# Sorted block attention and an FFN on one core: w_in in column halves, FFN1 pairs, a new order of the loads and of all engines' lists

## The chip, the cores and the metric

One core of one Trainium2 chip. The metric is the device time of one execution in microseconds; for the kernel before it is the median of three runs. All times in the timeline are counted from the start of the profiled span.

## The reference

`q`, `k` and `v` are `[4, 8, 768, 64]`, `sort_net` is `[4, 8, 8, 8]`. Each head's 768 tokens are 8 blocks of 96.

```python
P = sort_net
for _ in range(5):                       # row softmax, then column scaling
    P = np.exp(P - P.max(-1)); P = P / P.sum(-1); P = P / P.sum(-2)
k_sorted = einsum('bhij,bhjcd->bhicd', P, k_blocks)   # blocks mixed by P
v_sorted = einsum('bhij,bhjcd->bhicd', P, v_blocks)
attn = softmax(q_block @ k_sorted_block.T / 8)        # 96 x 96, block by block
x = (attn @ v_sorted_block)              # -> [3072 tokens, 512]
h = x @ w_in                             # w_in [512, 2048]
g = max(h, 0) + alpha * min(h, 0)
out = g @ w_out                          # w_out [2048, 512], float32
```

## The kernel before

The kernel is written as a graph of some 1,220 operations (`G.add`, with the engines that may run each, a planned duration, and the keys that it reads and writes). An order of all of them is written out by hand in the string `SEQ`; `arrange` walks through it, gives each operation its engine (the first that is allowed, or the one that a letter names: `d` for VectorE, `p` for GpSimd) and its place in that engine's list, and `emit` writes one program for each engine with the semaphore waits that the keys ask for. An entry such as `i15Y` puts 15 filler matmuls (`warm`, L1017: the identity times itself, 512 columns, into a PSUM bank that nobody reads) into TensorE's list. What stands behind a waiting instruction in an engine's list waits too.

The attention works on 32 groups `g` of 96 tokens (batch `g // 8`, block `g % 8`), all 8 heads at once. For batch 0 all preparation is done at the start:

- `load_q`, `load_k`, `load_v` go out on GpSimd's DMA queue, which also casts to bf16; then w_in (L931, four loads, one for each 128 rows), w_out (L936, two halves), and the k, v and q of batch 1 (`KS`, `VST`, `QN`).
- `sinkhorn` on VectorE, with one exponential on ScalarE in each of five rounds, makes `Pb`; `spread0` makes from it the block matrix `BDK` that mixes k and v of batch 0. `spread` makes `BDM` and `BDV` for batches 1 to 3 (L603, L613).
- `prep_q`, `prep_k` and `prep_v` are TensorE matmuls (L628, L703; for batches 1 to 3 L657 and L698) and a copy out of PSUM each (L400). Ahead of `prep_v` stand eight copies `conv_v` that regroup v; for later batches `conv_k` (L644) and `conv_v` copy into the zero-padded `KSz` and `VDz`.

In `attention(g)` there follow the scores (L741, L744), their negative maximum (L750, VectorE), the second scores with the maximum taken off (L765, L756), the exponential (L788, or L777 for batches 1 to 3, whose weights are turned by a DMA), the product with v (L797), reciprocal and scaling on VectorE (L805, L808), and the turn into `xT` (L823, or a DMA).

The FFN works on chunks of tokens: groups (0, 2) and (2, 4), 192 tokens each, then chunks of four groups, 384 tokens. `ffn1` computes one of 16 blocks of 128 hidden columns: four matmuls (L847), a negated relu into `t1` on ScalarE (L857) and a multiply-add into `hT` on VectorE (L860). Two PSUM banks (`psH`) take turns, and for the first chunk a third (`psYP`). `ffn2` (L886) sums over 16 `hT` tiles for 128 tokens, in four parts; a copy into `outstg` and a store follow.

Of the kernel before, what the change touches and what calls it, by code (L numbers as in the profile page):

```python
# [7 lines left out]
AP = bass.AP  # L8
# [24 lines left out]
0 2 11 7 3 4 1 8 9 i15Y 22 42 28 14 43 44 45 46 19 47 18 48 5 49 50 51 15 39 52 53 54 6 55 56 57 25 58 29 59  # L33
23 60 61 12 62 63 64 132 65 66 37 31 67 89 68 83 32 69 81 13 70 84 87 71 91 10 88 85 i8Y 72 40 73 90 130 74 75
86 76 133 41 77 82 78 131 92 79 i2Y 134 80 93 138 102 94d i2Y 103 26 104 147 95 105 100 148 96d 98 i4Y 99 24
101d 38 35 111a 113 97d 17 107d i2Y 158 149 106a 108d 21 159 146 i2Y 114 118 115 116 135 160 119 144 109a 124
143 125d 117 150 110a i3Y 136 145 112a i2Y 122 141 120 161 121d 30 20 123 140 36 i3Y 128 126 129d 142 151 127
137 16 139 162 152 163 164 i3G 153 165 154 183 155 166 184 i1P 167 156 157 33 i2Y 185 168 34 169 192 186 195
170 198 193 171 204 174 194 205 201 187 202 196 206 203 199 188 200 219 197 207 216 27 189 213 220 237 217 221
214 190 218 228 191 215 225 238 208 226 222 209 223 227 239 229 210 246 234 224 240 211 247 230 231 212d 235  # L40
260 253 236 290 261 241 232 248 250 242 272 262 251 249 233 291 269 252 254 270 263 350 172 255 243 292 264
271 256 258 265 293 244 312d 278 311 273 279 259d 303 337 280 266 257 245d 284 338 267 281 300 285 294 268 339
299 286 282 310 402 283 313 295 301 296 401 340 287 274 302d 304 288 314 289 347 297 309 305 315 316 298d 319
306d 317 346 341 320 378 318 307 321 322 342 308 379 325 275 323 351 324 177 343 348 326 328 175 380 327 329
355 179 349d 344 331 330 276 352 176 345d 334 381 178 353d 372 332 335 333 382 356 336 360 383 357 389 363 384
373 361 364 354 362 390 365 387 366 388d 393 385 369 367 359 386d 391 368 358 418 392 428 419 370 403 374 429
371 445 420 395 431 396d 375 430 394d 397 376 434 449 452 432 435 377 404 421 448 453 398d 436 405 447 454 181
433 399 444 458 400d 464 437 459 455 465 450 456 406 460 180 479 466 457 482 446 451d 422 182 461 423 478 483
424 476 462 407 484 467 475 477 463 494 408 474 480 495 485 481 425 504 548 486 426d 496 487 509 506 438 507d
491 505 439 488 440 492 497 535 510 493 489 524 511 441 490 515 508 442 525 512 516 534 536 517 513 468 549  # L50
414 526 469 470 521 412 514 471 537d 518 417 522 527 472d 538 523 410 519 498 560 539 499 520 545 411 409 500
542 277 546 413 561 501 540 543 550 416 502 544 562 547 415 554 541d 557 570 551 555 571 563 558 556 572 574
552 596 559 578 573 575 597 528 607 579 605 529 581 598 427 606d 608 590 530 576 580 443 591 577 582 609 583
531 625 599 637 532 584 626 610 636 564 585 587 611 569 565 627 566 634 612 592 586 635d 567 613 588 628 638
589 614 593 568 615 553 616 639d 594 503 619 617 600 620 640 601 595 661 618 641 473 621 622 602 658 623 603
676 659 645 604d 662 677 643 663 642 624 678 644 629 667 630 631 664 668 660 703 669 665 670 704 666 673 671
533 173 691 674 705 675 692 672 688 713 632 685 706 689 633d 690 712 693 686 679 687 700 717 718 701 697 714
702 694 698 715 699 723 695 748 719d 720 696 724 716 738 721 749 739 732 750 647 725 648 733 740 722 649 753
680 646 754d 729 747 681 726 741 682 730 767 776 731 727 707 734 768 683 781 735 728 769 777 708 709 778 755
751 736d 758 756 770 812 802 757 759 787 760 752 710 761 803 780 764 762 788 846 763 765 804 657 766 789 779d  # L60
651 793 653 742 805 794 782 743 784 744 654 790 795 785 745 656 783 786 771 837 791 772 650 813 773 796 838
655 774 799 797 814 825 652 798 800 792 811 815 839 801 826 816d 847 822 853 819 823 840 849 872 824 820 806
848 817 821 827 711 818 873 831 807 834 808 832 828 833 835 874 836 850 854 829d 883 857 851d 882 866 855 875
852 858 856 841 859 880 900 684 881 842 860 901 884 861 863 843 910 746 885 867 862 864 887 902 865 908 886
844 888 909d 911 891 868 889 903 892 912 893 876 913 869 809 877 890 878 914 897 915 737 894 870 879 898 934
# [10 lines left out]
1147 1142 1138 1143 1144 1151 1148 1152 1139 1153 1149 1150 1157 1140d 1220 1158 1154 1141 1159 1181 1155 1156  # L76
# [234 lines left out]
def bass_sinkhorn_attn__then__act_prelu_kernel(  # L311
# [26 lines left out]
    ANY = ("pool", "act", "dve")  # L338

# [237 lines left out]
    def spread(bs, prio):  # L577
# [24 lines left out]
        for x, b in enumerate(bs):  # L602
            G.add(DVE, lambda e, x=x, b=b: e.tensor_tensor(  # L603
                out=AP(BDM, b * 64, [[256, 128], [16, 4], [2, 8], [1, 2]]),
                in0=AP(mkhM, 0, [[8, 128], [2, 4], [0, 8], [1, 2]]),
                in1=AP(dsel, x * 8, [[48, 128], [0, 4], [1, 8], [0, 2]]), op=AluOpType.mult), 220,
                r=["dsel", "mkhM"], w=[("BDM", b)], prio=prio) if late else G.add(DVE, lambda e, x=x, b=b: e.tensor_tensor(
                out=AP(BDK, b * 128, [[512, 128], [16, 8], [2, 8], [1, 2]]),
                in0=AP(mkh, 0, [[16, 128], [2, 8], [0, 8], [1, 2]]),
                in1=AP(dsel, x * 8, [[48, 128], [0, 8], [1, 8], [0, 2]]), op=AluOpType.mult), 260,  # L610
                r=["dsel", "mkh"], w=[("BDK", b)], prio=prio)
        for x, b in enumerate(bs if late else []):
            G.add(DVE, lambda e, x=x, b=b: e.tensor_tensor(  # L613
                out=AP(BDV, b * 64, [[256, 128], [8, 8], [1, 8]]),
                in0=AP(mkhV, 0, [[8, 128], [1, 8], [0, 8]]),
                in1=AP(dsel, (n + x) * 8, [[48, 128], [0, 8], [1, 8]]), op=AluOpType.mult), 220,
# [102 lines left out]
    def attention(g, prio):  # L719
# [82 lines left out]
        if g == 1:  # L802
# [5 lines left out]
        G.add(DVE, lambda e: e.tensor_tensor(  # L808
            out=AP(xq[me], 0, [[512, 96], [256, 2], [64, 4], [1, 64]]),
            in0=AP(psZ, 0, [[1024, 96], [512, 2], [68, 4], [1, 64]]),  # L810
            in1=AP(rec[m], 0, [[8, 96], [4, 2], [1, 4], [0, 64]]), op=AluOpType.mult), t_dve(512),
            r=banks_o + [("rec", m)], w=[("xq", me)], prio=prio)
# [24 lines left out]
    def ffn1(ga, gb, ft, prio):  # L837
# [5 lines left out]

        def f(e):
            inst = None
            for kt in range(KT_TILES):
                inst = e.matmul(AP(pt, poff, [[1024, 128], [1, n]]),  # L847
                                AP(w_in_bf, kt * DFF + ft * 128, [[KT_TILES * DFF, 128], [1, 128]]),
                                AP(xT, kt * XR + tok % XR, [[KT_TILES * XR, 128], [1, n]]),
                                start=(kt == 0), stop=(kt == KT_TILES - 1))  # L850
            return inst
# [208 lines left out]
```

## Time and profile before

| what | value |
|---|---|
| median of the runs | 237.73 us (237.51 to 239.61) |
| the profiled execution | 238.1 us, span 236.4 us |
| TensorE, VectorE, ScalarE, GpSimd busy | 96%, 71%, 67%, 42% |
| granted TensorE clock | 1.0 |
| loads, size each: k, w_in, w_out, v of batch 1 | 768 KB x1, 512 KB x4, 1024 KB x2, 384 KB x2 |
| first FFN1 matmul | 29.82 us |

In the lines of the timeline the first two numbers are the start and the length; a group of matmuls has its count at the end, and in brackets stands the idle time before it and what ended it ("issue": nothing that the profile shows). Lengths of matmuls overlap, so the spacing of their starts is what one costs. PEld is the load of weights ahead of a matmul. The `q0` lines are the loads that GpSimd issues, `q8` is the queue that brings TensorE's program.

### The profile page before, as it was taken

The page shows a single profiled execution, that of the slowest core. Times are in us where ns is not written, and L with a number is a line of the kernel's source. Part 1 is how long each engine was busy: PE and PEld are TensorE (multiplying, and loading weights), DVE is VectorE, ACT ScalarE, POOL GpSimd, SP SyncE. Part 2 cuts the span into 40 slices and gives each one's busy share as a digit, 9 for nine tenths or more (in the row PEclk, how much of TensorE's full clock was granted, in tenths as well). Part 3 has the DMA queues.
Part 4 walks back from the last instruction along what each step waited for, and adds up shares of the span by engine and source line. Part 5 has one row for each costly group of instructions (what it writes and reads, how often), then busy time and mean ns, then how long its engine had stood idle before and what let it go on. Part 6 is the DMA issues. An engine that isn't in the chain of part 4 may idle for free.

```text
span 236.4 us, 6202 instructions
## 1 busy us (share of the span) xinstructions
PE 227.3 (96%) x2483; PEld 141.6 (60%) x2513; DVE 167.4 (71%) x343; ACT 158.7 (67%) x429; POOL 99.0 (42%) x144
## 2 busy tenths in 40 slices
PE   7898989999999999999999999999999999999995
PEld 3455677777666756655656565556555555555553
DVE  4764789998899988776888777566777667554420
ACT  4579456688989898676767778777676783543332
POOL 7989507934679995308999534000000000000000
PEclk9999999999999999999999999999999999999999
DMA  5999999995697998998889967594445222310023
GB/s 96 212 207 214 169 219 197 179 190 120 115 181 137 85 210 137 185 183 179 147 133 113 167 70 150 131 145 104 94 137 131 63 50 50 137 42 2 0 101 124
DMA packets 71981, 31.36 MB, mean 133 GB/s; under 512 B 64512, under 2 KB 67344, under 8 KB 71952
## 3 DMA queue, kind: packets, MB, share of 16 engines
q0 software_dynamic: 23408, 13.63, 44.3%
q1 hardware_dynamic: 48544, 17.33, 36.2%
q8 instruction: 20, 0.33, 0.6%
q14 instruction: 9, 0.07, 0.1%
HBM read 27.28 MB, written 6.29 MB: 142 GB/s over the span
## 4 chain that ended last, share of the span: by engine, by line
PE 85%; DMA 5%; ACT 4%; DVE 2%; POOL 2%; issue 2%; POOLq 0%
PE psH L847 34%; PE psYP L886 30%; DMA VST<-in_v_dram 5%; PE psS L886 4%; PE psS L741 4%; PE psO L797 3%; PE psYP L698 2%; PE psYP L657 2%; ACT hT L400 2%; PE psS L756 2%; PE psS L765 1%; PE psO L823 1%; ACT VS L400 1%; POOL VDz L484 1%; DVE nm L750 1%
## 5 line engine op out<-in xcount | busy, mean ns | idle before, releaser
L860 DVE SCALAR_TENSOR_TENSOR hT<-t,omaT,psH 128x384 bf16<-128x384 f32 (+1 forms) x139 | 77.3, 570 | 35.6 <-ACT t L857 34.4
L847 PE MATMUL psH<-xT,w_in_bf 128*128 128x384 bf16 (+1 forms) x556 | 97.9, 310 | 0.5 <-DVE rec L805 0.5
L857 ACT ACTIVATE t<-psH 128x384 f32<-128x384 f32 (+1 forms) x139 | 62.6, 462 | 41.9 <-PE psH L847 39.1
L886 PE MATMUL psYP<-w_out_bf,hT 128*128 128x512 bf16 x308 | 78.6, 379 | 1.6 <-issue 0.2
L847 PEld LDWEIGHTS psH<-xT,w_in_bf 128*128 128x128 bf16 x556 | 49.1, 98 | 29.3 <-DVE hT L860 2.3
L886 PEld LDWEIGHTS psYP<-w_out_bf,hT 128*128 128x128 bf16 x336 | 31.4, 98 | 29.7 <-ACT outstg L400 0.2
L777 ACT ACTIVATE Esb<-psS,nf 96x96 bf16<-96x96 f32 x192 | 46.2, 344 | 4.0 <-DVE nf L750 4.0
L400 POOL COPY VDz<-VST 64x384 bf16<-64x384 bf16 x40 | 33.9, 847 | 20.0 <-PE psYP L698 9.8
L644 POOL COPY KSz<-KS 64x512 bf16<-64x512 bf16 x36 | 22.1, 615 | 18.2 <-DMA KS<-in_k_dram 9.2
L750 DVE TENSOR_REDUCE nf<-psS 96x8 f32<-96x768 f32 x24 | 22.8, 951 | 4.1 <-PE psS L741 3.6
L808 DVE TENSOR_TENSOR xq<-psO,rec 96x512 bf16<-96x512 f32 x31 | 21.3, 688 | 0.7
L429 POOL DMA_DIRECT2D QN<-in_q_dram x24 | 19.8, 858 | 0.3 <-POOL QN L489 0.3
L400 ACT ACTIVATE outstg<-psYP 128x512 f32<-128x512 f32 x18 | 10.8, 598 | 5.3 <-PE psYP L886 5.1
L1017 PE MATMUL psYP<-identb 128*128 128x512 bf16 x46 | 13.3, 420 | 0.7 <-ACT identb L400 0.7
L797 PEld LDWEIGHTS psO<-VS,ET 112*128 112x128 bf16 x248 | 11.0, 98 | 3.4 <-ACT ET L788 0.3
L741 PEld LDWEIGHTS psS<-KT,QTz 128*96 128x96 bf16 x192 | 11.5, 125 | 2.1 <-ACT Esb L777 0.2
L797 PE MATMUL psO<-VS,ET 112*128 112x65 bf16 x248 | 12.7, 194 | 0.0
L741 PE MATMUL psS<-KT,QTz 128*96 128x96 bf16 x192 | 12.6, 208 | 0.0
L400 DVE CAST VS<-psYP 112x512 bf16<-112x512 f32 x15 | 10.3, 689 | 3.0 <-PE psYP L703 2.1
L698 PEld LDWEIGHTS psYP<-BDV,VDz 128*128 128x128 bf16 x192 | 8.3, 98 | 3.1 <-DVE VS L400 0.3
L805 DVE RECIPROCAL rec<-psO 96x8 f32<-96x8 f32 x31 | 6.2, 201 | 5.3 <-PE psO L797 5.2
L698 PE MATMUL psYP<-BDV,VDz 128*128 128x64 bf16 x192 | 9.5, 193 | 0.0
(139 smaller groups left out, 201.5 us busy)
## 6 DMA issues: line engine op xcount, KB each, us to landing
out_dram<-outstg SPq DMA_DIRECT2D x23, 256.0 KB, 2.4
KS<-in_k_dram POOLq DMA_DIRECT2D x3, 768.0 KB, 7.7
QN<-in_q_dram POOLq DMA_DIRECT2D x24, 96.0 KB, 6.0
w_in_bf<-in_moe_w_in_dram POOLq DMA_DIRECT2D x4, 512.0 KB, 11.2
w_out_bf<-in_moe_w_out_dram POOLq DMA_DIRECT2D x2, 1024.0 KB, 23.3
VST<-in_v_dram POOLq DMA_DIRECT2D x4, 384.0 KB, 16.0
hT<-in_q_dram POOLq DMA_DIRECT2D x1, 768.0 KB, 7.0
VST<-in_v_dram POOLq DMA_DIRECT2D x1, 768.0 KB, 10.7
```

The source lines that it names most:

```text
L400: return e.activation(o, i, ACTF.Copy) if e is nc.scalar else e.tensor_copy(o, i)
L644: G.add(POOL, lambda e, hp=hp: e.tensor_copy(AP(KSz, hp * 64 * 3072 + u % 3 * 1024 + hp * 64, [[3072, 64], [128, 8], [1, 64]]), AP(KS[n], ...
L698: inst = e.matmul(AP(t, off + dd * 64, [[row, 128], [1, 64]]), AP(VDz, (u % VSL * 8 + dd) * 128, [[VSL * 1024, 128], [1, 128]]), AP(BDV, b ...
L741: inst = e.matmul(o, AP(QTz[n], hp * 3072 + h4 * 768 + i * 96, [[6144, 128], [1, 96]]), AP(KT[n], (h4 * 8 + i) * bk, [[ld, 128], [64, 2], ...
L750: G.add(DVE, lambda e: e.tensor_reduce(AP(nx, 0, [[8, 96], [4, 2], [1, 4]]), AP(psX, 0, [[1024, 96], [512, 2], [96, 4], [1, 96]]), AxisLis ...
L777: inst = e.activation(AP(Esb[me], p * 128, [[1024, 96], [64, 2], [1, 48]]), AP(psX, (p // 4) * 512 + (p % 4) * 96, [[1024, 96], [48, 2], [ ...
L797: inst = e.matmul(AP(psZ, hp * 512 + h4 * 68, [[1024, 128], [1, 65]]), AP(ET[me] if far else ET[m], pos(h4, hp) * 96, [[800, nk], [1, 128] ...
L808: G.add(DVE, lambda e: e.tensor_tensor(out=AP(xq[me], 0, [[512, 96], [256, 2], [64, 4], [1, 64]]), in0=AP(psZ, 0, [[1024, 96], [512, 2], [ ...
L847: inst = e.matmul(AP(pt, poff, [[1024, 128], [1, n]]), AP(w_in_bf, kt * DFF + ft * 128, [[KT_TILES * DFF, 128], [1, 128]]), AP(xT, kt * XR ...
L857: G.add(ACT, lambda e: e.activation(AP(t1[tb], 0, [[384, 128], [1, n]]), AP(pt, poff, [[1024, 128], [1, n]]), ACTF.Relu, scale=-1.0), t_ac ...
L860: G.add(DVE, lambda e: e.scalar_tensor_tensor(out=AP(hT, ft * RING + tok % RING, [[FT_TILES * RING, 128], [1, n]]), in0=AP(t1[tb], 0, [[38 ...
L886: inst = e.matmul(AP(bank[0], bank[1], [[1024, 128], [1, n]]), AP(hT, ft * RING + tok % RING, [[FT_TILES * RING, 128], [1, 128]]), AP(w_ou ...
```

## The change

- `w_in` is still loaded in four pieces, but each is half of the columns of two row blocks (4 KB runs in place of 8 KB). An FFN1 block waits for the two pieces of its column half only.
- In chunks (0, 2) and (2, 4) an FFN1 operation computes two blocks side by side in one PSUM bank: eight matmuls, one relu over 384 columns, two multiply-adds over 192. 32 operations become 16.
- The products that make `BDM` and `BDV` may run on GpSimd; the new list puts two BDM and one BDV there.
- The scaling of the attention output may run on ScalarE; the new list leaves all 32 on VectorE.
- `SEQ` is new throughout. On GpSimd's queue both halves of w_out now follow w_in directly, ahead of batch 1's k. 27 fillers (`i15Y`, `i8Y`, `i4Y`) stand ahead of `prep_q` on TensorE, where 15 stood; there are 48 in all, before 46.

```diff
 SEQ = """
-0 2 11 7 3 4 1 8 9 i15Y 22 42 28 14 43 44 45 46 19 47 18 48 5 49 50 51 15 39 52 53 54 6 55 56 57 25 58 29 59
...
+0 2 11 7 3 4 1 8 22 9 42 28 i15Y 14 43 44 45 46 19 47 18 48 5 49 50 51 15 39 52 53 54 6 i8Y 55 56 57 25 58 29
+59 23 60 61 12 i4Y 62 63 64 10 130 65 66 40 67 131 81 68 85 69 82 83 21 70 i2Y 71 24 72 91 73 132 17 89 74 92
...
+    SMALL = ("dve", "pool")
...
-            G.add(DVE, lambda e, x=x, b=b: e.tensor_tensor(
+            G.add(SMALL, lambda e, x=x, b=b: e.tensor_tensor(
                 out=AP(BDM, b * 64, [[256, 128], [16, 4], [2, 8], [1, 2]]),
...
     def ffn1(ga, gb, ft, prio):
...
+        k = 2 if n == 192 else 1
         def f(e):
             inst = None
-            for kt in range(KT_TILES):
-                inst = e.matmul(AP(pt, poff, [[1024, 128], [1, n]]),
-                                AP(w_in_bf, kt * DFF + ft * 128, [[KT_TILES * DFF, 128], [1, 128]]),
+            for x in range(k):
+                for kt in range(KT_TILES):
+                    inst = e.matmul(AP(pt, poff + x * n, [[1024, 128], [1, n]]),
+                                    AP(w_in_bf, kt * DFF + (ft + x) * 128, [[KT_TILES * DFF, 128], [1, 128]]),
...
-        G.add(ACT, lambda e: e.activation(AP(t1[tb], 0, [[384, 128], [1, n]]),
-                                          AP(pt, poff, [[1024, 128], [1, n]]), ACTF.Relu, scale=-1.0),
+        G.add(ACT, lambda e: e.activation(AP(t1[tb], 0, [[384, 128], [1, k * n]]),
+                                          AP(pt, poff, [[1024, 128], [1, k * n]]), ACTF.Relu, scale=-1.0),
...
     for p in range(4):
         G.add(POOL, lambda e, p=p: e.dma_start(
-            AP(w_in_bf, p * DFF, [[KT_TILES * DFF, 128], [1, DFF]]),
-            AP(moe_w_in.tensor, p * 128 * DFF, [[DFF, 128], [1, DFF]])),
-            2550, w=[("w_in", p)], prio=-40 + p, dma=(dma_sem("wi%d" % p), 0))
+            AP(w_in_bf, p % 2 * 2 * DFF + p // 2 * 1024, [[KT_TILES * DFF, 128], [DFF, 2], [1, 1024]]),
+            AP(moe_w_in.tensor, p % 2 * 256 * DFF + p // 2 * 1024, [[DFF, 128], [128 * DFF, 2], [1, 1024]])),
+            2650, w=[("w_in", p)], prio=-40 + p, dma=(dma_sem("wi%d" % p), 0))
```

More of the change, by code (lines that the diff above doesn't have):

```diff
@@ L38 @@
[L38 to L42, printed above, removed]
@@ L807, in attention, with scaled @@
               r=banks_o, w=[("rec", m)], prio=prio)
[L808 to L812, printed above, removed]
+        def scaled(e):
+            if e is nc.vector:
+                return e.tensor_tensor(
+                    out=AP(xq[me], 0, [[512, 96], [256, 2], [64, 4], [1, 64]]),
+                    in0=AP(psZ, 0, [[1024, 96], [512, 2], [68, 4], [1, 64]]),
+                    in1=AP(rec[m], 0, [[8, 96], [4, 2], [1, 4], [0, 64]]), op=AluOpType.mult)
+            inst = None
+            for x in range(8):
+                inst = e.activation(AP(xq[me], x * 64, [[512, 96], [1, 64]]),
+                                    AP(psZ, x // 4 * 512 + x % 4 * 68, [[1024, 96], [1, 64]]),
+                                    ACTF.Copy, scale=rec[m][:, x:x + 1])
+            return inst
+        G.add(EITHER, scaled, {"dve": t_dve(512), "act": 1720},
+              r=banks_o + [("rec", m)], w=[("xq", me)], prio=prio)
         o2 = AP(xT, g * BLK % XR, [[KT_TILES * XR, 128], [XR, 4], [1, 96]])
@@ L852, in ffn1 @@
[L852 to L853 removed]
+            for x in range(k):
+                for kt in range(KT_TILES):
+                    inst = e.matmul(AP(pt, poff + x * n, [[1024, 128], [1, n]]),
+                                    AP(w_in_bf, kt * DFF + (ft + x) * 128, [[KT_TILES * DFF, 128], [1, 128]]),
+                                    AP(xT, kt * XR + tok % XR, [[KT_TILES * XR, 128], [1, n]]),
+                                    start=(kt == 0), stop=(kt == KT_TILES - 1))
@@ new lines, in ffn1 @@
+        for x in range(k):
+            G.add(DVE, lambda e, x=x: e.scalar_tensor_tensor(
+                out=AP(hT, (ft + x) * RING + tok % RING, [[FT_TILES * RING, 128], [1, n]]),
+                in0=AP(t1[tb], x * n, [[384, 128], [1, n]]), scalar=AP(omaT, ft + x, [[16, 128], [1, 1]]),
+                in1=AP(pt, poff + x * n, [[1024, 128], [1, n]]), op0=AluOpType.mult, op1=AluOpType.add),
+                t_dve(n) + 52, r=keys + [("t1", tb), "omaT"],
+                w=[("hT", ft + x, y % (RING // 64)) for y in range(tok // 64, (tok + n) // 64)], prio=prio)
```

91 lines of the change are left out of this document (48 added, 43 removed), and 17 rows, old and new, of the table SEQ.

## The prediction

> **What bounds the kernel now.** I read the page first, then busy times by stretches, then the timeline of TensorE's start, then the loads.
>
> ```profile
> span 236.4 us, 6202 instructions
> PE 227.3 (96%) x2483; PEld 141.6 (60%) x2513; DVE 167.4 (71%) x343; ACT 158.7 (67%) x429; POOL 99.0 (42%) x144
> 30.00:40.00 10.00, 9.26 (x149) 7.65 (x149) 8.80 (x24) 6.40 (x18) 3.32 (x6) 1.00 1.16 209
> 40.00:50.00 10.00, 9.85 (x151) 7.80 (x153) 9.74 (x23) 7.05 (x16) 8.52 (x13) 1.00 1.76 189
> 50.00:60.00 10.00, 9.74 (x146) 7.62 (x148) 9.02 (x23) 8.68 (x18) 3.58 (x5) 1.00 0.73 128
> 100.00:110.00 10.00, 9.95 (x76) 5.73 (x76) 7.12 (x13) 6.83 (x23) 2.88 (x4) 1.00 1.08 204
> ```
>
> TensorE is busy for 96% of the span, and from 100 us on it hardly pauses (9.95 of 10). The columns of a stretch are PE, PEld, DVE, ACT and POOL busy, then clock, DMA share and GB/s. Between 30 and 60 us VectorE is nearly as full as TensorE (8.80, 9.74, 9.02). Work that both kernels do alike in the long second part cannot give much. To see what can, I add up TensorE's work from the first FFN1 matmul at the spacing of matmul starts: 384-wide 0.1625 us (four in 0.65), 512-wide 0.215, 192-wide 0.0835.
>
> ```profile
> L847 PE MATMUL psH<-xT,w_in_bf 128*128 128x384 bf16 x448 | 85.4, 326 | 0.5 <-DVE rec L805 0.5
> 61.04 0.81 PE L847 MATMUL psH<-xT,w_in_bf 128*128 128x384 bf16 x4
> 61.69 0.59 PE L886 MATMUL psYP<-w_out_bf,hT 128*128 128x512 bf16 x2
> 59.29 0.81 PE L847 MATMUL psH<-xT,w_in_bf 128*128 128x384 bf16 x4
> 32.72 0.41 PE L765 MATMUL psS<-QTz,KT 64*112 64x96 bf16 x8 [0.37 <-DVE nm L750]
> 135.28 1.46 PE L847 MATMUL psH<-xT,w_in_bf 128*128 128x384 bf16 x8 [0.46 <-DVE rec L805]
> 231.75 1.91 PE L886 MATMUL psS<-w_out_bf,hT 128*128 128x256 bf16 x16
> ```
>
> By the lists that is 448 x 0.1625 = 72.8, 128 x 0.0835 = 10.7, 368 x 0.215 = 79.2, 32 x 0.108 = 3.5 and 33.4 for the small matmuls: 199.6 us in both kernels. The stream runs from 29.82 to 233.5 (16 of 0.108 after 231.75), 203.7. So pauses take 4.1 us: 0.4 at 30.95, 2.4 between there and the first 384-wide block at 59.29 (28.3 us for 25.9 of work, the score and maximum chain of batch 0 above all), 0.6 at 135.28, the rest in crumbs. The change can win at most these and what it takes from the start.
>
> **The start is paced by TensorE's own code.** Two pauses there wait for no semaphore:
>
> ```profile
> 2.81 3.38 PE L1017 MATMUL psYP<-identb 128*128 128x512 bf16 x8 [0.73 <-ACT identb L400]
> 5.34 2.35 PE L1017 MATMUL psYP<-identb 128*128 128x512 bf16 x9
> 8.38 0.44 PE L628 MATMUL psS<-identb,hT 64*64 64x64 bf16 x16 [0.69 <-DMA hT<-in_q_dram]
> 10.02 1.90 PE L1017 MATMUL psYP<-identb 128*128 128x512 bf16 x8
> 16.86 0.42 PE L744 MATMUL psS<-KT,QTz 64*96 64x96 bf16 x8
> 22.98 0.22 PE L703 MATMUL psO<-BDK,hT 128*64 128x64 bf16 x2 [0.35 <-issue]
> 29.82 0.83 PE L847 MATMUL psH<-xT,w_in_bf 128*128 128x192 bf16 x8
> 30.95 0.41 PE L847 MATMUL psYP<-xT,w_in_bf 128*128 128x192 bf16 x3 [0.22 <-issue]
> q0 software_dynamic: 146, 0.80, 100.2%
> q8 instruction: 1, 0.02, 27.9%
> q0 software_dynamic: 235, 0.83, 106.9%
> q8 instruction: 1, 0.02, 2.7%
> q0 software_dynamic: 640, 0.91, 108.9%
> q8 instruction: 1, 0.02, 2.4%
> ```
>
> [...] From 22.98 to 30.95 the rows count 125 matmuls, two instructions each, and a few waits: one block. Counting one block back from 22.98 gives 16.9 (in L744), two give 10.5 (in the fillers of L1017). [...] Entries: 10.5, 16.9, 23.0, 31.0.
>
> **The change, part by part.**
>
> *More fillers ahead of q.* 27 identity matmuls in place of 15 stand ahead of q's transposes. The first eight start 0.427 us apart (3.41 for eight), the later ones 0.215. They end at 2.81 + 3.41 + 19 x 0.215 = 10.3, while q was there at 8.38: +1.9 us. In the new list the second block is entered in the last group of q's transposes, 1.8 us after their begin: 12.1 in place of 10.5.
>
> *Code blocks.* The same number of matmuls stands ahead of FFN1 (592 for 593), so the later entries lie at the same places. From 12.1: 3.9 + 2.4 gives 18.4 for the next (16.9 before), 4.0 + 2.3 gives 24.7 (23.0), and, as the third lies behind w_in and then w_out, 5.2 + 2.4 gives 32.3 (30.95). Ends: 31.0, with the waits 0.4 shorter each time, and 33.6, with 5.5 on the last two bar 0.4. I take 32.3: **+1.35**.
>
> *Sinkhorn, k and v of batch 0.* The list puts ScalarE's fifth exponential behind a copy of q.
>
> ```profile
> 10.12 0.24 ACT L549 ACTIVATE P<-P 32x64 f32<-32x64 f32 x1
> 12.39 0.29 DVE L571 TENSOR_TENSOR BDK<-mkh,psYP 128x128 bf16<-128x128 f32 x1 [0.47 <-PE psYP L567]
> 16.50 1.61 ACT L400 ACTIVATE hT<-VST 128x384 bf16<-128x384 bf16 x2 [0.24 <-DMA VST<-in_v_dram]
> 16.50 0.99 DVE L400 COPY hT<-VST 128x384 bf16<-128x384 bf16 x2
> 16.61 1.56 POOL L400 COPY hT<-VST 128x384 bf16<-128x384 bf16 x1 [0.97 <-DMA VST<-in_v_dram]
> ```
>
> The copy waits for the transposes of 10.3 to 10.6 and takes 0.5, so the exponential slides from 10.12 to 11.25, and BDK behind it from 12.4 to 13.6. That is covered by v, which lands at 16.5 whatever happens, and by the code entry at 18.4; without these it would cost 1.2. Of the eight v copies ScalarE had five (0.81), VectorE two (0.5) and GpSimd one (1.56); now one, five and two: 4 x 0.81 leave ScalarE, 3 x 0.5 come to VectorE, and the attention of the first two groups could end 2 to 3 us sooner. The code waits take that: 0 here. The two GpSimd copies end by 19.8, ahead of their use.
>
> *w_in in halves, w_out ahead of k.*
>
> ```profile
> L931 POOL DMA_DIRECT2D w_in_bf<-in_moe_w_in_dram x4: 528/533/548, 8.2 to 11.8; - x4
> DMA to landing us min/median/max: 9.9/11.2/14.3
> 36.37 3.96 POOL L644 COPY KSz<-KS 64x512 bf16<-64x512 bf16 x6 [9.16 <-DMA KS<-in_k_dram]
> ```
>
> All of w_in is there by 11.8 + 14.3 = 26.1, ahead of 29.82; halves win nothing unless FFN1 starts sooner than that: 0. Behind w_in the queue carried w_out's first half (1024 KB) and batch 1's k (768 KB), and k was there at 36.4: 10.3 us for 1792 KB. So w_out's second half, now ahead of k, takes 10.3 x 1024 / 1792 = 5.9 and k comes at 42.3. Its first use in the new list stands 14.3 us of TensorE work behind the block entry, at 46.6 or later; two copies of 0.66 end at 43.6: 3.0 us of cover, 0; a k later than that costs what it is later. All bytes up to q's are the same, so batch 1's q lands as before. GpSimd's two BDM products stand ahead of seven q issues until VectorE's selection is ready near 31; until v's halves have followed k, about 46, the queue does not run dry: 0.
>
> *Pairs, and work moved off VectorE, 30 to 60 us.*
>
> ```profile
> L857 ACT ACTIVATE t<-psH 128x192 f32<-128x192 f32 x27 | 8.1, 328 | 2.9 <-PE psH L847 2.1 <-DVE hT L860 0.6
> L857 ACT ACTIVATE t<-psH 128x384 f32<-128x384 f32 x112 | 54.6, 495 | 39.0 <-PE psH L847 37.0 <-DVE hT L860 0.7
> L860 DVE SCALAR_TENSOR_TENSOR hT<-t,omaT,psH 128x192 bf16<-128x192 f32 x26 | 10.0, 406 | 1.1 <-ACT t L857 0.7
> L400 DVE CAST KT<-psYP 128x512 bf16<-128x512 f32 x3 | 2.0, 683 | 0.0
> L400 DVE CAST VS<-psYP 112x512 bf16<-112x512 f32 x3 | 2.1, 689 | 0.1
> ```
>
> Pairs save ScalarE 32 x 0.328 - 16 x 0.495 = 2.6 us; VectorE's 32 products stay, at a spacing of 0.37. Off VectorE ahead of its last 192-wide product go three KT and three VS casts (4.1), half of the BDM and BDV products (0.7) and odd copies, about 6 of 34 us. But the new list also asks sooner: that point comes after 22.9 us of TensorE work in place of 25.3, and VectorE, by the row means of its new list, has 27.9 us from group 2's maximum to that point, of which some 3.3 fit ahead of the block entry: 24.6 are left. It still decides: I take 2.0 us of pauses for 2.4, **-0.4** (from -1.9, its wait gone, to +1.0, pairs holding a bank longer).
>
> *The rest.* The pause at 135.28 may go or another come: **-0.1** (-0.6 to +1.5).
>
> Sum: +1.35 - 0.4 - 0.1 = +0.85. The profiled execution took 238.1 (236.4 of span and 1.7 around it), so 238.9 on its scale; it lies 0.4 above the median of the runs, 237.7, so 238.6. One per cent, 2.4 us, is about what a measurement of this kernel can tell from no change.
>
> **Rivals.** *Code is no brake (faster).* With waits of 2 us or less the v copies' 2 to 3 us come through: FFN1 could start at 27.0 and enter the next block at 27.7 in place of 30.95, -3.25; with -0.4 and -0.1 that is 234.0. For it: all else in the start is ready sooner. [...] The 0.35 us pause without a semaphore at 22.98 speaks against it in this stretch.
>
> *Code waits lengthen (slower).* [...] If the waits are 4.3, 5.5 and 5.5 us with 2.5 after each, the entries fall at 18.9, 26.9 and 34.9: +3.95, and with VectorE's -0.4 and -0.1 the time is 241.2. It decides (over 1% slower) from a mean wait of about 4.9 us on. [...]
>
> *The change does nothing it says (same).* The loads are hidden and the new order gives back in one place what it takes in another: 237.7.
>
> **Chances.** The forecast and the rival of nothing, both within 1%: 0.48. Code no brake 0.17, code waits lengthen 0.35 (with any other new stall of that size). Hence faster 0.17, same 0.48, slower 0.35. With one term at its end at a time the forecast's own range is 237.1 to 240.2; with all low it is 235.3. The range takes in most of both rivals: 235.0 to 242.2.
>
> **What would show it.** Right: q's transposes at 10.3 behind 27 fillers; pauses put down to issue near 18, 24 and 32 us; FFN1's second block not before 31; VectorE over 9 of 10 from 33 to 55; KSz copies from about 42.3. Wrong: FFN1 running on without a pause before 29.5; a wait for k, v or w_out's semaphore on TensorE; a pause of over 1 us after 60.

## The result, and the profile after

The changed kernel takes 250.16 us (median of four runs, 247.02 to 250.99) against 238.07 us for the kernel before (four runs): a ratio of 1.0463 with a 95% interval of 1.0409 to 1.0516. It is slower, and outside the predicted range of 235.0 to 242.2. The mean granted clock of the changed kernel is 0.979 to 0.986 in all four; the profiled execution is the one of 250.99 us, which counts as a slow run though its clock is that of two others, and as the ratios here leave slow runs out, 1.0463 is not the quotient of the two medians.

The page of the changed kernel: span, busy times, the granted clock in 40 slices (6.2 us each), and the lines on the chain that ended last.

```profile
span 249.3 us, 6214 instructions
PE 232.6 (93%) x2512; PEld 143.8 (58%) x2512; DVE 166.7 (67%) x340; ACT 154.7 (62%) x411; POOL 102.9 (41%) x149
PEclk9999999999999956999999999999999999999999
...
PE psH L859 31%; PE psYP L899 26%; PE psYP L1031 5%; DMA ET<-Esb 5%; PE psS L899 3%; PE psS L741 3%; PE psO L797 3%; PE psYP L698 2%; PE psYP L657 2%; DMA out_dram<-outstg 2%; PE psS L756 2%; DVE hT L873 1%; PE psO L832 1%; PE psS L765 1%; PE psS L744 1%
```

A transfer stands on the chain with 5%: the transposed scores `ET<-Esb`. The clock falls in the two slices of 87 to 99 us. Busy times by stretches (us; PE, PEld, DVE, ACT, POOL, then clock, DMA share, GB/s) show both places:

```profile
30.00:40.00 10.00, 9.89 (x159) 8.22 (x159) 8.95 (x24) 5.33 (x10) 6.53 (x11) 1.00 1.18 213
40.00:50.00 10.00, 10.00 (x156) 8.25 (x153) 8.98 (x23) 6.34 (x12) 7.47 (x12) 1.00 1.76 185
50.00:60.00 10.00, 9.81 (x148) 7.47 (x146) 9.01 (x22) 9.19 (x17) 8.00 (x13) 1.00 1.07 145
...
80.00:90.00 10.00, 4.88 (x42) 2.66 (x39) 4.33 (x9) 5.58 (x20) 9.42 (x14) 0.86 1.52 170
90.00:100.00 10.00, 8.29 (x74) 5.32 (x75) 4.23 (x9) 4.42 (x13) 1.24 (x2) 0.63 1.30 123
```

From 30 to 60 us, where the change was meant to act, TensorE is at least as full as before (9.89, 10.00, 9.81). From 80 to 90 it works for 4.88 of 10 us, and after that it runs at a clock of 0.63. The timeline of TensorE names the pause, and shows the start:

```profile
2.79 8.90 PE L1031 MATMUL psYP<-identb 128*128 128x512 bf16 x27 [0.72 <-ACT identb L400]
11.63 0.44 PE L628 MATMUL psH<-identb,hT 64*64 64x64 bf16 x16
...
20.34 0.29 PE L744 MATMUL psH<-KT,QTz 64*96 64x96 bf16 x4 [2.22 <-issue]
26.35 0.30 PE L756 MATMUL psH<-identb,nm 96*112 96x96 bf16 x2 [1.27 <-issue]
32.48 0.83 PE L859 MATMUL psH<-xT,w_in_bf 128*128 128x192 bf16 x8
...
91.71 0.60 PE L797 MATMUL psO<-VS,ET 112*128 112x65 bf16 x8 [6.83 <-DMA ET<-Esb]
```

The matmul of group 11 (the expectations below call a group a block row) stood 6.83 us until its transposed scores had landed. Adding up TensorE's work as the prediction did (199.6 us from the first FFN1 matmul on, in both kernels), the whole difference of the spans, 249.3 - 236.4 = 12.9 us, divides into four (rounded):

| part, us | before | after | difference |
|---|---|---|---|
| first FFN1 matmul | 29.82 | 32.48 | +2.7 |
| pauses from there to 84 us | 3.1 | 2.8 | -0.3 |
| pauses from 84 us on, with the slow clock | 1.0 | 10.8 | +9.8 |
| from the last matmul's start to the end | 3.0 | 3.8 | +0.8 |

Of the 9.8, 7.0 are the pause from 84.9 to 91.7 and 2.7 the matmuls at the low clock up to 100 us; the rest is 0.1. These are sums from one profiled execution of each kernel.

**What the transposes stood behind.** The timeline of GpSimd's and SyncE's queues in the changed kernel:

```profile
75.26 0.90 POOL L429 DMA_DIRECT2D QN<-in_q_dram  x1
76.15 0.56 POOL L447 DMA_DIRECT2D KS<-in_k_dram  x1
76.69 4.14 POOL L429 DMA_DIRECT2D QN<-in_q_dram  x5
...
78.62 1.44 SPq L913 DMA_DIRECT2D out_dram<-outstg  x3
80.10 7.72 SPq L782 DMA_TRANSPOSE ET<-Esb  x3
```

The tile `ET` from 76 to 96 us, three transposes, from issue to landing:

```profile
DMA to landing us min/median/max: 9.9/11.2/11.5
```

The DMA queues from 78 to 92 us (packets, MB, share of 16 engines):

```profile
q0 software_dynamic: 2747, 1.07, 93.5%
q1 hardware_dynamic: 1985, 1.17, 52.0%
```

The same timeline of the kernel before:

```profile
59.74 0.58 POOL L447 DMA_DIRECT2D KS<-in_k_dram  x1
77.83 6.58 POOL L429 DMA_DIRECT2D QN<-in_q_dram  x8
...
74.94 6.11 SPq L782 DMA_TRANSPOSE ET<-Esb  x2
81.10 1.30 SPq L900 DMA_DIRECT2D out_dram<-outstg  x2
85.22 1.22 SPq L782 DMA_TRANSPOSE ET<-Esb  x1
```

and its tiles, from issue to landing, first the one k load of 59.74, then `ET` from 74 to 96 us:

```profile
DMA to landing us min/median/max: 6.9/6.9/6.9
...
DMA to landing us min/median/max: 2.8/2.9/4.7
```

Before, batch 2's k (768 KB) went out at 59.74, and two stores went out between one transpose and the next. The new order issues k at 76.15, behind the first of batch 2's eight q loads, and puts three stores of 256 KB directly ahead of three transposes. From 78 to 92 us the packets of queue 0 (GpSimd's loads) took 93.5% of the 16 engines' time and those of queue 1 (stores and transposes) 52%, which is more than the whole, so they lay on top of each other. The three transposes took 9.9 to 11.5 us; before, transposes took 2.8 to 4.7, the long ones among the q loads.

### The profile page after: what moved, and what is told of

Its sections match the earlier page's. It is cut to its first block, busy times and chain, and to the rows that moved or that the text cites. A ratio compares the mean times of both kernels' runs of the same rounds, so it can differ in the third digit from the quotient of the medians.

```text
span 249.3 us, 6214 instructions
## 1 busy us (share of the span) xinstructions
PE 232.6 (93%) x2512; PEld 143.8 (58%) x2512; DVE 166.7 (67%) x340; ACT 154.7 (62%) x411; POOL 102.9 (41%) x149
## 4 chain that ended last, share of the span: by engine, by line
PE 86%; DMA 6%; DVE 3%; issue 2%; ACT 1%; POOL 0%; POOLq 0%; SPq 0%; ACTq 0%
PE psH L859 31%; PE psYP L899 26%; PE psYP L1031 5%; DMA ET<-Esb 5%; PE psS L899 3%; PE psS L741 3%; PE psO L797 3%; PE psYP L698 2%; PE psYP L657 2%; DMA out_dram<-outstg 2%; PE psS L756 2%; DVE hT L873 1%; PE psO L832 1%; PE psS L765 1%; PE psS L744 1%
## 5 line engine op out<-in xcount | busy, mean ns | idle before, releaser
L873 DVE SCALAR_TENSOR_TENSOR hT<-t,omaT,psH 128x384 bf16<-128x384 f32 (+1 forms) x140 | 75.8, 567 | 34.0 <-ACT t L869 33.2
L859 PE MATMUL psH<-xT,w_in_bf 128*128 128x384 bf16 (+1 forms) x560 | 97.5, 312 | 0.4 <-DVE hT L873 0.2
L869 ACT ACTIVATE t<-psH 128x384 f32<-128x384 f32 x126 | 61.4, 494 | 47.4 <-PE psH L859 46.4
L899 PE MATMUL psYP<-w_out_bf,hT 128*128 128x512 bf16 x336 | 83.5, 382 | 0.5 <-ACT outstg L400 0.5
L859 PEld LDWEIGHTS psH<-xT,w_in_bf 128*128 128x128 bf16 x560 | 49.8, 98 | 28.2 <-DVE hT L873 3.0
L797 PE MATMUL psO<-VS,ET 112*128 112x65 bf16 x248 | 12.9, 195 | 6.8 <-DMA ET<-Esb 6.8
L400 ACT ACTIVATE VS<-psYP 112x512 bf16<-112x512 f32 x16 | 11.0, 690 | 11.5 <-PE psYP L698 7.7
L797 PEld LDWEIGHTS psO<-VS,ET 112*128 112x128 bf16 x248 | 11.2, 99 | 11.2 <-issue 7.3
L1031 PE MATMUL psYP<-identb 128*128 128x512 bf16 x45 | 14.3, 458 | 0.7 <-ACT identb L400 0.7
L805 DVE RECIPROCAL rec<-psO 96x8 f32<-96x8 f32 x31 | 6.2, 200 | 11.2 <-PE psO L797 11.0
L741 PEld LDWEIGHTS psS<-KT,QTz 128*96 128x96 bf16 x192 | 12.1, 127 | 2.5 <-ACT Esb L777 0.2
L741 PE MATMUL psS<-KT,QTz 128*96 128x96 bf16 x192 | 12.9, 211 | 0.0
L400 ACT ACTIVATE outstg<-psYP 128x512 f32<-128x512 f32 x13 | 7.7, 600 | 6.9 <-PE psYP L899 5.0
L698 PE MATMUL psYP<-BDV,VDz 128*128 128x64 bf16 x192 | 10.0, 197 | 0.0
## 6 DMA issues: line engine op xcount, KB each, us to landing
w_in_bf<-in_moe_w_in_dram POOLq DMA_DIRECT2D x4, 512.0 KB, 13.8
VST<-in_v_dram POOLq DMA_DIRECT2D x1, 768.0 KB, 10.4
```

The lines of the kernel that those rows point to most:

```text
L400: return e.activation(o, i, ACTF.Copy) if e is nc.scalar else e.tensor_copy(o, i)
L698: inst = e.matmul(AP(t, off + dd * 64, [[row, 128], [1, 64]]), AP(VDz, (u % VSL * 8 + dd) * 128, [[VSL * 1024, 128], [1, 128]]), AP(BDV, b ...
L741: inst = e.matmul(o, AP(QTz[n], hp * 3072 + h4 * 768 + i * 96, [[6144, 128], [1, 96]]), AP(KT[n], (h4 * 8 + i) * bk, [[ld, 128], [64, 2], ...
L797: inst = e.matmul(AP(psZ, hp * 512 + h4 * 68, [[1024, 128], [1, 65]]), AP(ET[me] if far else ET[m], pos(h4, hp) * 96, [[800, nk], [1, 128] ...
L859: inst = e.matmul(AP(pt, poff + x * n, [[1024, 128], [1, n]]), AP(w_in_bf, kt * DFF + (ft + x) * 128, [[KT_TILES * DFF, 128], [1, 128]]), ...
L869: G.add(ACT, lambda e: e.activation(AP(t1[tb], 0, [[384, 128], [1, k * n]]), AP(pt, poff, [[1024, 128], [1, k * n]]), ACTF.Relu, scale=-1. ...
```

## The experiments

In `SEQ` a number is an operation; moving it moves it on its engine's list and on no other. 371 is batch 2's k load, 378 to 385 its q loads, 377, 345 and 261 the stores of token tiles 2, 1 and 0, 465, 495 and 531 the transposes of groups 11 to 13. In the table the median is over all executions, and each ratio is to the kernel before as run in the same round (medians 238.07 to 238.77). The last three columns come from the profiled execution, which need not be the median one; the pauses are added up as above.

| kernel | median, us | ratio to before, 95% interval | first FFN1 | pauses after it | span |
|---|---|---|---|---|---|
| after | 250.16 | 1.0409 to 1.0516 | 32.48 | 13.6 | 249.3 |
| e1_k_early | 245.81 | 1.0240 to 1.0366 | 30.23 | 9.9 | 243.5 |
| e2_stores_late | 243.61 | 1.0165 to 1.0279 | 33.12 | 7.5 | 243.7 |
| e3_both | 239.84 | 1.0007 to 1.0070 | 30.95 | 4.2 | 238.2 |
| e4_fillers15 | 245.55 | 1.0264 to 1.0322 | 29.09 | 11.4 | 243.8 |
| e5_both_15 | 238.28 | 0.9978 to 1.0031 | 28.80 | 11.8 | 243.5 |
| e6_before_stall | 241.41 | 1.0102 to 1.0166 | 30.21 | 8.0 | 240.6 |
| e7_before_halves | 237.99 | 0.9973 to 1.0008 | 29.88 | 4.0 | 236.3 |
| e8_split_relu | 237.05 | 0.9920 to 0.9965 | 30.14 | 3.9 | 236.5 |
| e9_turns_later | 238.27 | 0.9981 to 1.0013 | 28.90 | 5.3 | 236.6 |
| e10_turns_27 | 240.60 | 1.0054 to 1.0105 | 30.57 | 5.0 | 238.0 |
| e11_k1_first | 238.24 | 0.9977 to 1.0010 | 28.67 | 4.7 | 235.8 |
| e12_last_waits | 235.95 | 0.9873 to 0.9906 | 28.63 | 3.4 | 234.4 |

**k of batch 2 back to 60 us.**

```diff
-480 463 394 371 406 481 461
+480 463 394 406 481 461
-341 179 329 326 398 401 420
+341 179 329 326 371 398 401 420
```

> The changed kernel with one entry moved: batch 2's k load (768 KB, GpSimd's queue) goes from its place among batch 2's q loads (issued 76.15 in the changed kernel's trace) to behind a VDz copy at about 60.6; everything else stays. Theory A (the load's bytes are what the score transposes of block row 11 wait behind): they were issued at 80.1 and landed at 91.58, the k load held the engines from about 77.5 to 84.51, so the transpose lands near 85.5 to 86.5, TensorE's pause of 6.83 us falls to under 1.5 us, the granted clock no longer falls to 0.63 after it, and the time falls by about 8 us, to 241 to 243. Theory B (the three output stores ahead of the transposes on SyncE's queue are what counts): they still land one after the other over 3 us, the pause stays above 4 us and the time at 246 to 249. Theory C (the eight q loads of 256-byte packets are what counts): the same as B, the transpose shares the engines with them whatever k does, 246 to 249.

TensorE's pause in the timeline, the landing of `ET` (74 to 96 us), and two stretches:

```profile
86.54 0.41 PE L796 MATMUL psO<-VS,ET 112*128 112x65 bf16 x8 [3.91 <-DMA ET<-Esb]
```

```profile
DMA to landing us min/median/max: 4.4/6.2/8.6
```

```profile
80.00:90.00 10.00, 6.09 (x66) 3.85 (x64) 4.46 (x8) 5.26 (x16) 7.90 (x11) 0.90 1.45 148
90.00:100.00 10.00, 10.00 (x103) 6.30 (x102) 7.90 (x16) 6.79 (x20) 2.45 (x4) 0.93 0.88 145
```

The median landing falls from 11.2 to 6.2 us, that of group 11's own transpose from 11.5 to 8.6, and the pause from 6.83 to 3.91 us: k counts for less than theory A said, and more than B and C did. The time, 245.81, lies just below what B and C expected.

**The stores behind the transposes.**

```diff
-410 377 492 485 381 487 345 436 493 449 489 261 378 465 516
+410 492 485 381 487 436 493 449 489 378 465 516
-472 479 531 469 564
+472 479 531 377 345 261 469 564
```

> The changed kernel with three entries moved: the output stores of token tiles 2, 1 and 0 (256 KB each, SyncE's queue) go from just ahead of the score transposes of block rows 11, 12 and 13 to just behind them. Theory A (k's bytes): the transposes still wait for the k load, which lands at about 84.5, and for their own 3 to 4 us, so the first lands at 88 to 89; the pause is 3 to 4 us, the clock still falls for a while, 244 to 247. Theory B (the stores): the first transpose lands before 86, the pause is under 1.5 us, 241 to 243. Theory C (the q loads): pause over 5 us, 247 to 250.

The same views:

```profile
87.23 0.41 PE L796 MATMUL psO<-VS,ET 112*128 112x65 bf16 x8 [1.71 <-DMA ET<-Esb]
92.29 0.41 PE L796 MATMUL psO<-VS,ET 112*128 112x65 bf16 x8 [1.37 <-DMA ET<-Esb]
```

```profile
DMA to landing us min/median/max: 2.8/7.8/9.0
```

```profile
90.00:100.00 10.00, 8.63 (x99) 5.54 (x98) 7.81 (x15) 6.36 (x18) 3.75 (x7) 1.00 1.01 167
```

Two short pauses are left of the long one, and the clock stays at 1.00 behind them; the time, 243.61, lies between what A and B expected. Neither k nor the stores alone are the cause.

**Both.** The two edits above together.

> The moves of the two kernels before together: k of batch 2 at about 60.6, the three stores behind the transposes. Theories A and B: the pause is under 0.7 us, no fall of the clock, 240 to 242, which leaves the later start (2.5 us) against the fewer pauses from 33 to 60 as what the changed kernel still differs by. Theory C (the q loads alone hold the transposes): the pause stays over 3 us, 244 or more.

The landing of `ET`, 74 to 96 us:

```profile
DMA to landing us min/median/max: 2.9/3.9/5.8
```

The transposes land in 2.9 to 5.8 us, the pause is gone, and the pauses after the first FFN1 matmul add up to 4.2 us against 4.1 before. The eight q loads (theory C; 4,063 packets of 0.51 MB on queue 0 from 78 to 92 us, some 125 bytes each), which are still there, cost no pause. The stall of the changed kernel is therefore k and the stores in front of the transposes: of its 13.6 us of pauses the move of k alone takes 3.7 away, that of the stores alone 6.1, and both together 9.4, so the two nearly add up, and the stores weigh more (by the medians 4.4, 6.6 and 10.3 us). The median, 239.84, is a little below the 240 to 242 expected; the ten executions range from 238.37 to 242.36.

**The fillers.**

```diff
-53 54 6 i8Y 55 56 57
+53 54 6 55 56 57
-60 61 12 i4Y 62 63 64
+60 61 12 62 63 64
```

> The changed kernel with 15 instead of 27 filler matmuls ahead of the first q transposes (two entries, of 8 and of 4, left out; the fillers compute nothing that is used). The stall at 85 to 92 stays, so only the start is priced. Theory S (the fillers hold the start): the q transposes begin at about 9.1 instead of 11.63, the first FFN1 matmul at about 30 instead of 32.48, the time falls by 2 to 2.5 us. Rival R (the code fetches behind the loads set the pace from 18 us on, whatever happens ahead of them): the pauses at 20.34 and 26.35 grow by what the start gains, the first FFN1 matmul stays within 0.7 us of 32.5, and the time within 0.7 us.

TensorE's timeline:

```profile
2.79 4.78 PE L1030 MATMUL psYP<-identb 128*128 128x512 bf16 x15 [0.72 <-ACT identb L399]
29.09 0.83 PE L858 MATMUL psH<-xT,w_in_bf 128*128 128x192 bf16 x8
87.33 0.60 PE L796 MATMUL psO<-VS,ET 112*128 112x65 bf16 x8 [5.86 <-DMA ET<-Esb]
```

4.6 us less by the medians, where theory S expected 2 to 2.5. The stall is still there but shorter by 1 us, the pauses with the slow clock by 2.2, and the start is 3.4 us earlier than in the changed kernel's profile. Rival R is out. What the 12 fillers cost where no stall is in the way, e10 shows below.

**Both moves and 15 fillers**, the edits of the three kernels before together.

> The changed kernel with k of batch 2 at about 60, the three stores behind the transposes, and 15 instead of 27 fillers. With both moves alone the stream from the first FFN1 matmul on lost 4.18 us to pauses, before 4.11; the start was 30.95 against 29.82 and the tail 3.6 against 3.0. Theory (start, pauses and tail are all that differs): with 15 fillers the first FFN1 matmul comes at 29.1 as with 15 alone, the pauses stay at 4.2, the tail at 3.6, so the span is about 236.3 and the time 237 to 238.5, the same as before within 1%. Rival (an earlier start only brings the same waits on loads sooner): pauses grow by 1 us or more, 239 to 240.

The median is level with before, as expected. But only eight of the twelve executions took 237.25 to 238.93 us; three took 239.58, 240.64 and 243.11, and the profiled one 245.26: there the moved k load met other transposes. The landing of that k load, and TensorE's timeline:

```profile
DMA to landing us min/median/max: 13.8/13.8/13.8
```

```profile
74.10 0.62 PE L797 MATMUL psO<-VS,ET 112*128 112x65 bf16 x8 [4.79 <-DMA ET<-Esb]
```

Now group 8 waited: on SyncE's queue its transpose stands behind batch 1's q transposes, and these were under way together with k, which took 13.8 us. What the other three executions lost is in no profile.

**The stall made in the kernel before.** 403 is the k load there, 409 and 277 the stores, 527 the transpose of group 12.

```diff
-428 419 370 403 374 429
+428 419 370 374 429
-468 549 414 526 469
+468 549 414 403 526 469
-522 527 472d
+522 409 277 527 472d
-545 411 409 500 542 277 546
+545 411 500 542 546
```

> The kernel before with three entries moved the other way: batch 2's k load from 59.74 to behind the first of batch 2's eight q loads (about 78.6), and the stores of token tiles 2 and 0 from behind the score transpose of block row 12 to ahead of it. Nothing else of the change. Theory (order of the DMAs makes the stall, whatever the rest of the order): that transpose landed at 84.53 and its tile was used at 87.13; behind 768 KB and 512 KB more it lands 7 to 10 us later, so the pause is 4 to 7 us, the granted clock falls after it and the time rises to 243 to 248. Rival (the stall needs the changed kernel's bunching of all three transposes behind the loads; before's earlier ones keep it clear): pause under 1.5 us, 238 to 240.

TensorE's timeline, and the landing of `ET` from 74 to 96 us:

```profile
88.73 0.41 PE L657 MATMUL psYP<-BDM,KSz 128*128 128x64 bf16 x8 [2.50 <-POOL KSz L644]
```

```profile
DMA to landing us min/median/max: 2.8/8.5/10.0
```

The 2.8 is a transpose ahead of the loads; the two behind k and the stores land 10.0 and 8.5 us after their issue, against 9.9 to 11.5 in the changed kernel, so the order of the transfers alone makes them late. But TensorE's wait is another one, for GpSimd's copy of the late k; the mean clock stays at 1.00, and the time rises by 3 us, below the 243 to 248 expected. The late transposes came about, the stall on them did not. That its size depends on what else TensorE has to do ahead of the late tile is argued, not shown.

**w_in in halves alone**, in the kernel before:

```diff
-            AP(w_in_bf, p * DFF, [[KT_TILES * DFF, 128], [1, DFF]]),
-            AP(moe_w_in.tensor, p * 128 * DFF, [[DFF, 128], [1, DFF]])),
+            AP(w_in_bf, p % 2 * 2 * DFF + p // 2 * 1024, [[KT_TILES * DFF, 128], [DFF, 2], [1, 1024]]),
+            AP(moe_w_in.tensor, p % 2 * 256 * DFF + p // 2 * 1024, [[DFF, 128], [128 * DFF, 2], [1, 1024]])),
...
-  r=... [("w_in", kt) for kt in range(KT_TILES)]
+  r=... [("w_in", ft // 8 * 2 + x) for x in range(2)]
```

> The kernel before with w_in loaded in column halves, in the order of the changed kernel, and each FFN1 block waiting for its half alone; order and fillers stay. Theory (w_in has landed by 26.2 to 27.5 and the first FFN1 matmul comes at 29.82 for other reasons): no difference, 237 to 239.5. Rival (1.05 MB pieces of two row groups are read slower, or the earlier half frees FFN1): the first FFN1 matmul moves by over 0.7 us, and the time with it.

No difference, and the first FFN1 matmul at 29.88.

**The pair read by two ScalarE instructions**, on top of both moves and 15 fillers:

```diff
-        G.add(ACT, lambda e: e.activation(AP(t1[tb], 0, [[384, 128], [1, k * n]]),
-                                          AP(pt, poff, [[1024, 128], [1, k * n]]), ACTF.Relu, scale=-1.0),
+        G.add(ACT, lambda e: [e.activation(AP(t1[tb], x * n, [[384, 128], [1, n]]),
+                                          AP(pt, poff + x * n, [[1024, 128], [1, n]]), ACTF.Relu, scale=-1.0) for x in range(k)][-1],
```

> The kernel with both moves and 15 fillers, and the paired FFN1 blocks read by ScalarE in two instructions of 192 columns instead of one of 384 (16 more ScalarE instructions in the first two chunks); the PSUM pairing and TensorE's order stay. Theory (from 31 to 59 VectorE is at over 9/10 and ScalarE has room): nothing changes beyond 0.5 us. Rival (the single ScalarE instruction is what cut the pauses of 31 to 60 us): the pauses by 60 grow by 0.7 us or more, and the time with them.

Up to 60 us the pauses are 2.1 us in both: the rival is out. Yet its median is 1.2 us below that of e5, which neither theory said (six of its eight executions took 236.61 to 238.19, the others 240.71 and 242.79). Of this, 0.6 us lie behind the last matmul's start (3.5 us to the end in e5, 3.0 here); where the rest lies is open. DMA queues of the last 4 us in the changed kernel, then in this one:

```profile
q1 hardware_dynamic: 398, 0.45, 31.6%
q14 instruction: 1, 0.01, 1.1%
```

```profile
q1 hardware_dynamic: 543, 0.72, 49.4%
```

With 411 ScalarE instructions (after, e1 to e5) a packet of code is fetched beside the last store, whose 16 parts then land 0.7 to 1.1 us apart; with 427 or 429 (before, e6 to e12) there is none and they land within 0.2 us. That held in all 14 profiles, and is the size of the +0.8 us in the last row of the table of four parts. As e5 and this kernel differ in these sixteen instructions alone, it is their number that puts a code fetch beside the last store or takes it away.

**Three q transposes of batch 1 behind those of groups 8 and 9**, on top of e8:

```diff
-321 340 291 180 337 334
+321 340 291 337 334
-398 401 420 181 358d
+398 401 420 358d
-356d 362 182 424
+356d 362 424
-426 425 344d 389 402
+426 425 344d 389 180 181 402
-412 367 451 405 432
+412 367 451 405 182 432
```

> The kernel with both moves, 15 fillers and the two Relu instructions, with the last three q transposes of batch 1 moved on SyncE's queue: two from ahead of the score transpose of block row 8 to behind it, one behind that of block row 9. In the profile of both moves with 15 fillers the k load issued at 56.9 landed at 70.73, two q transposes at 71.16 and 73.45 and the score transpose at 74.05, after which TensorE lost 4.96 us; where the load landed at 67.38 the score transpose landed at 68.97 and nothing was lost. Theory (a transpose lands only when the load issued ahead of it has landed, and in SyncE's order): the score transpose of row 8 lands about 1.2 to 3.5 us earlier against the k load's landing, such losses are gone or under 1.5 us, 236 to 237.5. Rival (the moved q transposes hold up the score transposes of rows 9 and 10 or batch 2's q loads behind them): a new pause of over 1 us between 66 and 90, 237.5 or more.

TensorE's timeline:

```profile
84.33 0.39 PE L698 MATMUL psYP<-BDV,VDz 128*128 128x64 bf16 x8 [1.04 <-POOL VDz L400]
```

Theory and rival both came true in part: the losses of e5 are gone (twelve executions from 237.49 to 239.21), and the q loads of batch 2, which wait for the last of the moved transposes, came later and held GpSimd's v copies, 1.2 us by the spacing of starts. The median, 238.27, is the rival's, 1.2 us above e8: the edit bought evenness, not speed.

**The same with 27 fillers**, that is e9 without the fillers' edit.

> The same with 27 fillers instead of 15, as in the changed kernel; no stall is left that could blur the price of the start. Theory (the fillers end at 10.4 to 11.6 instead of 7.6 and the first code fetches come that much later): the first FFN1 matmul comes 1 to 3 us later than with 15, the time rises by 1 to 3 us, and the runs differ among themselves by 1 us or more as the fillers' own speed does. Rival (the code fetches behind the loads set the pace): within 0.5 us of the kernel with 15.

TensorE's timeline:

```profile
30.57 0.83 PE L859 MATMUL psH<-xT,w_in_bf 128*128 128x192 bf16 x8
```

240.60 against 238.27: twelve fillers cost 2.3 us by the medians, 1.7 at the first FFN1 matmul of these two profiles (30.57 against 28.90). The executions range from 239.62 to 243.36.

**k of batch 1 ahead of w_out's second half**, on top of e9:

```diff
-79 86 135 80 i2Y 93 138 95
+79 86 138 135 80 i2Y 93 95
```

> The kernel with the later q transposes and 15 fillers, with batch 1's k load issued ahead of w_out's second half, where the kernel before has it. Theory (neither is waited for): k lands near 36.5 and w_out's second half at about 41.5, no pause over 0.5 us appears before 60, the time stays within 0.7 us of the kernel with the later q transposes. Rival (the second half is needed by the first FFN2 tile, or k's copies were late): a pause appears or goes at 38 to 45 and the time moves by 1 us or more.

238.24 against 238.27: no difference, though k landed at 36.1 instead of 41.1 and its copies start at 39.11 instead of 41.21.

**The two waits left, by order alone**, on top of e9:

```diff
-460 393 480 463
+446 384 460 393 480 463
-488 490 446 494 437 491 510 438d 383 474 513 385 439
+488 490 494 437 491 510 438d 474 513 439
-475 518 473 515
+475 518 473 383 515
-468d 472 479
+468d 472 385 479
-1047 1013 892 1020
+1047 1013 1020
-1027 978 961 969
+1027 978 961 892 969
```

> The kernel with the later q transposes and 15 fillers, with two waits more taken out by order alone: on GpSimd's queue one VDz copy goes ahead of batch 2's q loads and the last two q loads go behind the next VDz copies (the v reordering matmul waited 1.20 us for them at 84.33); on SyncE's queue the store of token tile 11 goes from behind four transposes to ahead of two score transposes (its staging tile's next copy, and through it an FFN2 tile, waited 0.77 us at 189.09). Theory (both waits go and nothing comes in their place): the pauses from the first FFN1 matmul on fall from 5.27 to about 3.3 us, the time from 238.3 to 236 to 237, ratio to the kernel before 0.990 to 0.995. Rival (the q loads now land later and batch 2's q transposes hold up block row 16, or the store delays the score transposes behind it): a pause of 1 us or more at 95 to 110 or 175 to 190, 237.5 or more.

235.95 us, 0.9889 of the kernel before (0.9873 to 0.9906): about 1.1% faster than it, a little more than expected. Its page:

```profile
span 234.4 us, 6207 instructions
```

Against before's span, 236.4: 1.2 us from the first FFN1 matmul (28.63 against 29.82) and 0.7 from the pauses (3.4 against 4.1).

## Why the prediction was wrong

**The step that failed is "the rest".** It was sized at -0.1 us, at most +1.5, and measured +9.8 in the profile. The prediction followed the loads of batch 1 through the queues (w_out, k, v, q up to 50 us) and none of batch 2's, though the same new list moves k by 16.4 us, past VDz copies and into the q loads, and puts three stores ahead of three transposes on SyncE's queue. It wrote itself what would refute it, a pause of over 1 us after 60, and gave that no mechanism. Rows of before would have shown a pause, but not its size: k issued at 76.15 with before's 6.9 us lands at 83.05, a transpose of 2.9 to 4.7 us behind it at 86.0 to 87.8, and TensorE came to the tile at 91.71 - 6.83 = 84.9: 1.1 to 2.9 us of the 6.83. In fact k took 8.4 us, the three stores landed by 87.4, and the transpose only at 91.6.

**The fillers: right in kind, mis-sized.** 27 fillers were to end at 10.3 with eight at the slow spacing of 0.427 us; in the changed kernel they ended at 11.7. That eight was one execution's number: with 27 the fillers ended between 10.4 and 11.7 us in five profiles, and over all 14 the switch to 0.215 us fell after 7 to 14 matmuls. The windows of the profile show a granted clock of 1.00 for the slow matmuls too, but the records of the clock begin only at 5.6 to 8.8 us, where the spacing changes (one trace has none). (In all there are 48 fillers after and 49 before, not 46.)

**The code blocks: the mean close, in part by luck.** +1.35 us at the start was predicted; the five profiles of the changed order with 27 fillers (after, e1, e2, e3, e10) have the first FFN1 matmul at 30.23 to 33.12, on average 31.47, which is +1.65 on the one profile of before. In the profiled execution of the changed kernel it was +2.66, twice the term. Two pauses put down to issue came there, of 2.22 and 1.27 us, at 20.34 and 26.35, 1.9 and 1.7 later than said; in e1 to e3 the first came alone, and the third, near 32, came in none of the five. And three of the five starts hold something that the prediction did not have: behind the first code wait the clock fell to one half for 3.4 us. In e1 (two fillers take 1.03 us there, 0.60 at the full clock):

```profile
18.21 0.29 PE L743 MATMUL psH<-KT,QTz 64*96 64x96 bf16 x4 [1.40 <-issue]
21.26 1.03 PE L1030 MATMUL psYP<-identb 128*128 128x512 bf16 x2
```

Half a clock for 3.4 us is about 1.7 us of work (an estimate), so that without it the average would be near +0.6. That these pauses are waits for code is read from the q8 packets; no run tests it by itself. The sum put 3.9, 4.0 and 5.2 us from the entry of one block to the start of the next one's packet, and 2.3 or 2.4 from there to the next entry. No run shows these terms, nor that a packet is asked for at an entry; the traces show where packets start and pauses end. Before, packets start at 14.4, 20.7 and 28.5 us, the last two 2.2 and 2.5 ahead of the ends of the pauses at 22.98 and 30.95; in the changed kernel at 18.0, 23.9 and 30.1, the first two 2.3 and 2.4 ahead of the ends at 20.34 and 26.35. From such an end to the next packet it is 5.5 us before and 3.6 and 3.7 in the changed kernel, where the sum had 4.0 and 5.2. The 125 matmuls and as many weight loads of one block fit the page of before: 20 packets on q8 for 4,996 of them, some 250 to a packet (an estimate). The rival that code is no brake had FFN1 at 27.0; with 15 fillers the new order does start sooner (28.6 to 29.1 in five of six profiles; 30.14 in the other, e8, where the clock was halved from 24.3 to 27.7; 29.82 before), about a third of that. Pauses put down to issue, of 0.25 to 0.97 us, stay there too, and the 12 fillers more than spend the gain.

**VectorE, 30 to 60 us: right in size.** -0.4 was predicted; the pauses up to 84 us fell by 0.3 in one profile of each kernel, with VectorE at 8.95, 8.98 and 9.01 of 10. Two Relu instructions for one changed nothing there, so the gain does not come from the single Relu; whether pairing or VectorE's lighter list made it was not separated.

**w_in's halves, w_out ahead of k, BDM on GpSimd: right at 0.** e7 and e11 measured the first two. k was predicted for 42.3 and landed at 41.3. BDM on GpSimd had no run of its own.

**Missed and small:** +0.8 us at the end, from a code fetch beside the last store; the sum had no term for the end.

## What to carry to other kernels

When an order is searched anew, follow every large transfer that moves, in all batches, past each transfer that a compute engine waits for; put its time to landing against the slack of that wait. Stores that nobody waits for belong behind the transposes that somebody waits for (here 6.1 us of pauses, e2), and a bulk load where no transpose is due for its own length (3.7 us, e1). A pause can cost more than its length, since the clock may fall behind it: here 6.83 us cost 2.7 us more.

## What was not expected of the hardware

- The clock fell to one half for 3.4, 6.8 or 10.2 us at a time, by the traces' records of it: in the changed kernel from 87.2 to 97.5 us, behind the start of the pause of 6.83 us; in e4 from 84.1 to 90.9 (pause of 5.86), in e5 from 73.3 to 80.1 (4.79), in e1 from 88.0 to 91.4 (3.91). Pauses of 1.71 and 1.37 us in e2 were followed by 1.00. At the start, however, waits of 3.44 us in e2, 1.66 in e3, 1.40 in e1 and 0.97 in e8 were each followed by half the clock for 3.4 us, and one of 2.22 in the changed kernel was not. What decides there stays open.
- Transposes and stores share SyncE's queue, and both share the engines with GpSimd's loads (78 to 92 us of the changed kernel: 52% and 93.5% of the 16 engines' time): group 11's transpose took 4.6 us to landing with k and stores away (e3), 8.6 behind the stores (e1), 8.1 behind the k load (e2), 11.5 behind both (after). By what rule the engines are shared and landings ordered was not shown.
- In these 14 profiles sixteen ScalarE instructions more or fewer (411, or 427 and 429) decide whether a code fetch falls beside the last store: 0.7 to 1.1 us between its parts, or 0.2.
